# Issue order of the staged value stores, and the last output projection by heads, in a two-layer segment-memory transformer

## The chip, the cores and the metric

The kernel runs on one core of a Trainium2 chip. A core has four compute engines, each with its own instruction stream: PE (TensorE, matrix products into PSUM), DVE (VectorE), ACT (ScalarE) and POOL (GpSimd). A fifth engine, SP, does no arithmetic here: it issues most of the DMA transfers, one after the other. An instruction that waits for a semaphore holds up all that stands behind it on its own engine, and on no other. PE runs every product as a pair, a weight load (shown as PEld) and a matmul.

The metric is the device time of one execution in microseconds (us); shorter is better. The time before is 1611.96 us, the median of three runs (1608.64 to 1615.45).

## The reference

The input x has 2048 tokens of 512 features. Two layers, each applied twice in turn, make the output: A, a recurrent memory attention, and B, a dense block with ReLU, each behind a layer norm and with a residual.

```python
def _A_ref(x, mem0, Wq, Wk, Wv, Wo, seg_len):        # H=32 heads of 128, M=8, seg_len=32
    mem = mem0
    for s in range(n_seg):                             # 64 segments, one after the other
        h = concatenate([mem, xs], axis=1)             # 8 memory rows + 32 tokens
        q, k, v = h @ Wq, h @ Wk, h @ Wv               # per head
        p = softmax(where(mask, q @ k.T * scale, -1e9))
        o = (p @ v) summed over heads through Wo
        mem = o[:, :M, :]                              # the next segment's memory
        outs.append(o[:, M:, :])

x = x + A(layernorm(x), mem0, ...)
x = x + relu(layernorm(x) @ w1) @ w2                   # Dff = 1376
x = x + A(layernorm(x), mem0, ...)
x = x + relu(layernorm(x) @ w1) @ w2
```

The memory makes A sequential over its 64 segments. The second A needs the tokens of the first A and B only, so it may follow a few segments behind.

## The kernel before

**Steps.** One loop runs over steps k = 0 to 67 (`LAST`). Step k does segment k of the first A (k < 64) and segment k-4 of the second A (k >= 4, `DELTA`); B for the tokens of step k-2 is fitted in between. Steps 0 to 3 and 64 to 67 have one layer only (`single` in `step`); the others have both.

**Within a step.** For half of the heads `qk` makes queries and keys (L540, copied from PSUM by ACT at L546 and DVE at L548), `scores` (L574) and `softmax` (L590 to L606) follow, then the other half. `transpose_p` or a DMA transpose (`turn_p`, L623) turns the probabilities, `weighted_v` (L642) multiplies by the values in `Vs`, `output_mem` (L582) projects the memory rows, `new_memory` copies them (L774), turns them (L780) and hands them to the next step (`HTm` L791, `HT` L794). At the end `memory_values(k + 1)` makes the next step's values of the memory rows (L725), copies them (L729) and stores them.

**Values by way of DRAM.** The values of a segment's tokens do not depend on the memory and are made ahead, in `values0` (L314), `values_tile` (L354) and `memory_values` (L725). A product tile has heads across partitions, while `Vs` wants tokens there; so each tile is copied to SBUF (L320, L358, L729, all ACT), stored to DRAM in 128 KB pieces, and read back in the other layout (`load_values` L697 to L706, `load_memory_values` L735). The copies go to a ring of five SBUF buffers (tag `vst`): a copy must wait until the store of the copy five before it has landed.

**Step 0 and its staging.** Step 0 makes more value tiles than five buffers hold, while the weights still come in. It therefore puts 15 tiles into the space of the dense weights `w1_sb` and `w2_sb` (`slots` in `first_step`), which are loaded only in step 1 (`load_dense`, L157 to L160). The two stores of `vd_second` (L359), the values that step 1 needs, are issued at once. The other 13 go through `put(True, ...)`, which only appends them to the list `held`. Step 1 empties that list (L877) behind `load_memory_values` (L735) and ahead of its `load_dense`, which overwrites the staging space and so must wait for those stores.

**Order.** The streams of PE, DVE, SP and POOL are in the order in which the program is written. ACT's alone is arranged by a scheduler from its own estimates, so a change elsewhere can shift ACT's instructions.

**Output projection of the tokens.** `output_x(k)` multiplies the 32 token rows of all heads (`OTx`) by `Wo`. Four groups of 32 columns of the PE array work at once. In the quarter form (L401) the four groups take the four quarters of the 512 output columns of one head: 128 pairs of a weight load and a matmul of 128 columns. In the form by heads (L396, where `by_heads(k)` is true) they take two heads times two halves: 64 pairs with 256 columns each, and the two partial sums are added later: `add_output` then does four additions of 32x256 (L417) in place of four of 32x128 (L426). Before, `by_heads` is true for k = 0 to 2 and 63 to 65. The projection of step 67 is done after the loop, at the very end of the program, and has the quarter form.

Of the kernel before, what the change touches and what calls it, by code (L numbers as in the profile page):

```python
# [22 lines left out]
def kernel(  # L23
# [14 lines left out]
    nc = tc.nc  # L38
# [9 lines left out]
    LAST = NSEG + DELTA - 1  # L48
# [20 lines left out]
    def has0(k):  # L69
        return 0 <= k < NSEG  # L70

    def has1(k):
        return DELTA <= k <= LAST
# [30 lines left out]
    def load_xb(n):  # L104
        tag, bufs = ("vst", 5) if n in (1, 2, 3) else ("xb", 1)
        xbs[n] = wk.tile([128, Dm], BF, tag=tag, bufs=bufs, name="xb")
        nc.sync.dma_start(out=xbs[n][:], in_=A_x[0, 128 * n:128 * n + 128, :])
# [101 lines left out]
    for a in range(2):  # L209
        t = ps_s.tile([128, 512], F32, name=f"sp{a}")  # L210
# [4 lines left out]
    xT0, xnT_tiles, hT_tiles, vd0, vd1, vmds, wm_tiles, wo_tiles, xp_tiles, vp_tiles, obs = {}, {}, {}, {}, {}, {}, {}, {}, {}, {}, {}  # L215
# [9 lines left out]
    def normalize(eng, dst, src, mom, lo, hi):  # L225
        mv, rstd = mom
        eng.tensor_scalar(out=dst[lo:hi, :], in0=src[lo:hi, :], scalar1=mv[lo:hi, 0:1], scalar2=rstd[lo:hi, 0:1],
                          op0=ALU.subtract, op1=ALU.mult)

    def moments_x(n):  # L230
        stats = wk.tile([128, 6], F32, tag="ln_stats", bufs=1)
        nc.vector.bn_stats(out=stats[:], in_=xbs[n][:])
        return stat_tail(stats, "x")
# [47 lines left out]
    def layers(k):  # L281
        return [a for a in range(2) if (has0, has1)[a](k)]
# [10 lines left out]

    held = []

    def put(later, **store):
        if later:
            held.append(store)  # L300
        else:
            nc.sync.dma_start(**store)  # L302

    def values0(p, n, lo=0, hi=NC4, pool=None, stage=None):
        r = 64 * (p % 2)
        if (n, lo) == (0, 0):
            vd0[p] = dram.tile([4, 2, 64, 512], BF, tag="vd0", bufs=3, name="vd0")
        if lo == 0:
            pool, tag = (pool, "wo") if pool else (ps_fill, "fill")
            vp_tiles[p, n] = pool.tile([128, 512], F32, tag=tag, name="vp")  # L310
        vp = vp_tiles[p, n]
        for c4 in range(lo, hi):
            for j in range(2):
                nc.tensor.matmul(vp[64 * j:64 * j + 64, :], lhsT=xT0[p // 2][:, c4, r:r + 64],  # L314
                                 rhs=Wv_sb[:, c4, (n + j) * 512:(n + j + 1) * 512],
                                 start=(c4 == 0), stop=(c4 == NC4 - 1), tile_position=(0, 64 * j))
        if hi < NC4:
            return
        vst = wk.tile([128, 512], BF, tag="vst", bufs=5, name="vst")[:] if stage is None else stage
        nc.scalar.copy(out=vst, in_=vp[:])  # L320
        put(stage is not None, out=vd0[p][n // 2].rearrange("j t e -> (j t) e"), in_=vst)

    def values_first(ii):

# [78 lines left out]
                                     tile_position=(0, 32 * j))  # L403

    def by_heads(k):
        return k + 1 < LAST and len(layers(k + 1)) == 1

    def add_output(k, part=None):
        if not 0 <= k <= LAST or ox_span(k) is None:
# [306 lines left out]
    def memory_values(k, stage=(None, None), part=range(2)):  # L716
        if 0 in part:
            vmds[k] = dram.tile([2, 4, 32, 512], BF, tag="vmd", bufs=7, name="vmd")
        vmd = vmds[k]
        for ii in part:  # L720
            vp = ps_c.tile([128, 512], F32, tag="c", name="vm")
            for c4 in range(NC4):
                for j in range(4):
                    n = 4 * ii + j
                    nc.tensor.matmul(vp[32 * j:32 * j + 32, :], lhsT=HTm[:, c4, :],  # L725
                                     rhs=Wv_sb[:, c4, n * 512:(n + 1) * 512],
                                     start=(c4 == 0), stop=(c4 == NC4 - 1), tile_position=(0, 32 * j))
            VmS = wk.tile([128, 512], BF, tag="vst", bufs=5, name="VmS")[:] if stage[ii] is None else stage[ii]
            nc.scalar.copy(out=VmS, in_=vp[:])  # L729
            put(k == 0, out=vmd[ii].rearrange("j t e -> (j t) e"), in_=VmS)  # L730

    def load_memory_values(k, act):
        for ii in range(2):
# [23 lines left out]
    def split(k):  # L757
        return len(values_at(k)) in (2, 3)
# [90 lines left out]
    def step(k):  # L849
        act = layers(k)  # L850
        single = len(act) == 1
        cont = [a for a in act if k - DELTA * a + 1 < NSEG]
        n_x = k // 4 + 3
        has_x = n_x < NXT
        by_pe = k in (1, LAST)
        ahead = has1(k + 1) or not cont
        if k % 4 == 0 and has_x:
            load_xb(n_x)
        with tc.high_priority(offset=PRIO):
            behind = norm_rows.pop(k, None)  # L860
            if k == 1:
                def behind():
                    normalize(nc.vector, xbs[n_x], xbs[n_x], moments_x(n_x), 0, 128)
            qks = qk(0, act, behind=behind)
            load_values(k, act)
            if k == 1:
                memory_values(k)
                inputs_T(n_x, True)
        part = 4 if k == LAST else 8 if single else 5
        mid = 8 if k == LAST else 16  # L870

        light = split(k)
        block(k, 0, part)
        with tc.high_priority(offset=PRIO):
            transpose_step(k)
            load_memory_values(k, act)
            while held:  # L877
                put(False, **held.pop(0))
            scores(qks, act)
            softmax(0, act, by_pe)  # L880
            if not by_pe:
                turn_p()
        if k % 4 == 3 and has_x:
            inputs_T(n_x)
        if has0(k + 1):
            load_x(k + 1)
        if k == 1:
            load_dense()
        with tc.high_priority(offset=PRIO):
            qks = qk(1, act)  # L890
        if single:
            block(k, part, mid)
        elif light:
            dense_h(k - 2, slice(0, 1))
            block(k, part, 16)
        else:
            dense_h(k - 2)
        with tc.high_priority(offset=PRIO):
            scores(qks, act)
            softmax(1, act, by_pe)  # L900
        if single:
            dense_h(k - 2, slice(0, 1) if k == LAST else slice(None))
            block(k, mid, H)
        elif light:
            dense_h(k - 2, slice(1, None))
            block(k, 16, H)
        else:
            block(k, part, H)
        f_mid = 9 if ahead or k == 2 else 5
        if k < LAST:  # L910
            dense_y(k - 2, 0, f_mid)
        if not single:
            add_output(k - 1)
        if k % 4 == 1 and k > 1 and has_x:
            mom["x"] = moments_x(n_x)
        with tc.high_priority(offset=PRIO):
            transpose_p(1)
        if ahead and k < LAST:
            dense_y(k - 2, f_mid, NFC)
        tokens_in(k + 1)  # L920
        if k < LAST and spare_T(k + 1) is not None:
            nc.gpsimd.tensor_copy(out=HTm[:, :, 2 * M:32], in_=spare_T(k + 1))
        with tc.high_priority(offset=PRIO):
            pvs = weighted_v(act)
            outputs(k, pvs)
        if single and k < LAST and ahead:
            add_dense(k - 2)
            store(k - 2)
        if single:
            add_output(k - 1, 0)  # L930
        if cont:
            with tc.high_priority(offset=PRIO):
                pool, tag = (ps_c, "c") if single else (ps_wo, "wo")
                wo = pool.tile([128, Dm], F32, tag=tag, name="wo")
                output_mem(k, wo)
        if not ahead:
            dense_y(k - 2, f_mid, NFC)
        if not single and k < LAST and ahead:
            add_dense(k - 2)
            store(k - 2)  # L940
        if cont:
            with tc.high_priority(offset=PRIO):
                new_memory(k, cont, wo)
        if single:
            add_output(k - 1, 1)
        if not ahead:
            add_dense(k - 2)
            store(k - 2)
        values1(k + 1, 1)
        if cont:  # L950
            output_ride(k)
            with tc.high_priority(offset=PRIO):
                memory_values(k + 1)
        with tc.high_priority(offset=PRIO):
            prepare(k + 1)
        if k % 4 == 2 and k > 2 and has_x:
            normalize(nc.vector, xbs[n_x], xbs[n_x], mom["x"], 0, 128)

    mom = {}
    with tc.manual_schedule(engines={mybir.EngineType.PE, mybir.EngineType.DVE, mybir.EngineType.SP,  # L960
# [30 lines left out]
        t = xnT_tiles[d + 2] = wk.tile([128, NC4, 128], BF, tag="xnT", bufs=1, name="xnT")  # L991
# [48 lines left out]
```

## Time and profile before

| what | value |
|---|---|
| median of three runs | 1611.96 us (1608.64 to 1615.45) |
| the profiled execution's own time | 1608.92 us |
| its span, first to last instruction | 1607.2 us |
| mean granted TensorE clock | 0.995 |
| PE busy | 1570.6 us, 98% of the span, 42782 matmuls |
| DVE / ACT / POOL busy | 1262.9 / 738.7 / 347.6 us |
| DMA moved | 146.39 MB, mean 91 GB/s |

The span is 1.7 us shorter than the execution's own time. PE is close to always busy over the whole, so a saving can lie only where PE waits, or where PE's work itself shrinks. The timeline gives the start and length of each instruction or run of instructions, in us from the start of the span; a bracket behind a row says how long the engine had been idle and what ended that. In the chain of waits each row is a piece of the path that ended last.

### The profile page before, as it was taken

Reading aid. Unit: us, or ns where it says so; the run is one execution under the profiler, and the core shown is the slowest. Engines: PE = TensorE matmul, PEld = TensorE weight load, DVE = VectorE, ACT = ScalarE, POOL = GpSimd, SP = SyncE. Lnnn points to the kernel's source line nnn. Section 1 sums busy time; section 2 is a strip of 40 time slices with the busy share of each in tenths; the row PEclk is TensorE's granted clock in tenths of the full one; section 3 lists DMA queues with packets and bytes.
Section 4 is the critical chain, followed back from the end, with each engine's and each line's share of the span. In section 5 each row is a group of like instructions: output and inputs, shape, how many; then the busy total and the mean of one; then the engine's idle time right before and its main releaser. Section 6 shows DMA issues by size and latency. Waiting matters only on the chain.

```text
span 1607.2 us, 94867 instructions
## 1 busy us (share of the span) xinstructions
PE 1570.6 (98%) x42782; PEld 1324.2 (82%) x42782; DVE 1262.9 (79%) x3112; ACT 738.7 (46%) x1800; POOL 347.6 (22%) x666
## 2 busy tenths in 40 slices
PE   6889999999999999999999999999999999999997
PEld 4567888988898888889888888988888898888876
DVE  4468888888888888888888888888888888787765
ACT  3434445454544544454454545445454544545432
POOL 2012122222222222222222222222222222221210
PEclk9989999999999999999999999999999999999999
DMA  9634343444343355434433443343443333324232
GB/s 368 218 76 76 89 79 76 85 90 81 74 91 82 80 77 97 82 71 86 83 84 73 97 83 76 83 82 88 72 100 82 78 76 79 92 62 100 70 70 37
DMA packets 222533, 146.39 MB, mean 91 GB/s; under 512 B 123976, under 2 KB 216496, under 8 KB 222128
## 3 DMA queue, kind: packets, MB, share of 16 engines
q1 hardware_dynamic: 218976, 136.09, 38.3%
q8 instruction: 336, 5.51, 1.6%
q0 software_dynamic: 3072, 4.20, 1.1%
q14 instruction: 69, 0.57, 0.2%
q10 hardware_dynamic: 80, 0.03, 0.0%
HBM read 65.41 MB, written 45.35 MB: 69 GB/s over the span
## 4 chain that ended last, share of the span: by engine, by line
PE 94%; DMA 3%; SPq 1%; DVE 1%; issue 1%; ACT 0%; POOLq 0%; ACTq 0%; DVEq 0%
PE qp L540 37%; PE wox L373 10%; PE wo L582 8%; PE vm L725 7%; PE v L354 7%; PE hp L476 6%; PE sp L499 5%; PE pv L642 4%; PE sp L574 4%; PE vp L314 3%; DMA Wv_sb<-in_A_Wv_dram 2%; PE tp L616 1%; PE xp L447 1%; SPq L302 1%; DMA vd<-vst 0%
## 5 line engine op out<-in xcount | busy, mean ns | idle before, releaser
L546 ACT CAST QT<-qp 128x480 bf16<-128x480 f32 (+3 forms) x408 | 201.5, 494 | 395.7 <-PE qp L540 393.2
L540 PE MATMUL qp<-HT,Wk_sb 128*128 128x80 bf16 (+1 forms) x8704 | 369.8, 200 | 3.8 <-ACT VmS L729 2.3
L540 PE MATMUL qp<-HT,Wq_sb 128*128 128x80 bf16 (+1 forms) x8704 | 370.1, 200 | 2.4 <-POOL HT L714 1.2
L540 PEld LDWEIGHTS <-Wq_sb 128*128 128x128 bf16 x8704 | 326.2, 99 | 34.2 <-issue 26.7
L540 PEld LDWEIGHTS <-Wk_sb 128*128 128x128 bf16 x8704 | 328.9, 100 | 5.2 <-issue 4.0
L548 DVE CAST KT<-qp 128x480 bf16<-128x480 f32 (+3 forms) x408 | 225.3, 565 | 104.6 <-PE qp L540 102.3
L606 POOL TENSOR_TENSOR P_sb<-es,sm 128x320 bf16<-128x320 f32 x185 | 130.8, 721 | 753.4 <-ACT es L596 514.5
L373 PE MATMUL wox<-Wo_sb,OTx 128*64 128x256 bf16 x2880 | 173.8, 273 | 0.0
L590 DVE TENSOR_REDUCE mx<-sp 128x8 f32<-128x320 f32 x256 | 114.9, 487 | 74.1 <-PE sp L574 74.1
L601 DVE TENSOR_REDUCE sm<-es 128x8 f32<-128x320 f32 x256 | 118.9, 465 | 44.4 <-ACT es L596 34.0
L373 PEld LDWEIGHTS <-OTx 128*64 128x64 bf16 x2880 | 150.2, 110 | 3.1
L596 ACT ACTIVATE es<-es 128x320 f32<-128x320 f32 x256 | 110.5, 469 | 60.7 <-DVE es L594 59.9
L725 PE MATMUL vm<-Wv_sb,HTm 128*32 128x512 bf16 x2176 | 136.5, 380 | 0.6 <-DVE HT L794 0.6
L582 PE MATMUL wo<-Wo_sb,OTm 128*32 128x512 bf16 x2144 | 128.7, 380 | 0.0
L354 PE MATMUL v<-Wv_sb,xnT 128*32 128x512 bf16 x2048 | 128.7, 378 | 0.0
L566 DVE CAST sp<-maskb 128x320 f32<-128x320 bf16 x256 | 118.4, 484 | 0.0
L594 DVE TENSOR_TENSOR es<-sp,mx 128x320 f32<-128x320 f32 x256 | 113.8, 483 | 1.5
L725 PEld LDWEIGHTS <-HTm 128*32 128x32 bf16 x2176 | 91.0, 96 | 27.0 <-issue 12.4
L499 PE MATMUL sp<-w_sb,hT 128*64 128x256 bf16 (+4 forms) x1474 | 106.8, 278 | 0.5 <-ACT hT L482 0.5
L476 PE MATMUL hp<-xnT,w_sb 128*128 128x64 bf16 (+3 forms) x2948 | 102.8, 193 | 3.4 <-DMA xnT<-XN 2.4
L729 ACT CAST VmS<-vm 128x512 bf16<-128x512 f32 x134 | 78.6, 586 | 56.0 <-PE vm L725 53.9
L476 PEld LDWEIGHTS <-w_sb 128*128 128x128 bf16 (+1 forms) x2948 | 95.6, 101 | 4.5 <-issue 3.8
(113 smaller groups left out, 2026.4 us busy)
## 6 DMA issues: line engine op xcount, KB each, us to landing
Vs<-vd SPq DMA_DIRECT2D x96, 256.0 KB
vd<-vst SPq DMA_DIRECT2D x181, 128.0 KB
vmd<-VmS SPq DMA_DIRECT2D x134, 128.0 KB
Vs<-vmd SPq DMA_DIRECT2D x254, 32.0 KB
Vs<-vmd SPq DMA_DIRECT2D x60, 128.0 KB
Wq_sb<-in_A_Wq_dram SPq DMA_DIRECT2D x2, 2048.0 KB
Wk_sb<-in_A_Wk_dram SPq DMA_DIRECT2D x2, 2048.0 KB
Wv_sb<-in_A_Wv_dram SPq DMA_DIRECT2D x2, 2048.0 KB
```

Of the source, the lines that this page charges most:

```text
L354: nc.tensor.matmul(vp[32 * j:32 * j + 32, :], lhsT=tokens[:, c4, :], rhs=Wv_sb[:, c4, n * 512:(n + 1) * 512], start=(c4 == 0), stop=(c4 == ...
L373: nc.tensor.matmul(out[64 * j:64 * j + nr, 0:256], lhsT=lhsT, rhs=rhs[:, 256 * j:256 * j + 256], start=start, stop=stop, tile_position=(0, ...
L476: nc.tensor.matmul(hp[0:fs, fc - f0, 0:n], lhsT=w1_sb[:, c4, fc * 128:fc * 128 + fs], rhs=cols(c4), start=(c4 == 0), stop=(c4 == NC4 - 1))
L499: nc.tensor.matmul(sp_banks[bank][64 * j:64 * j + n, 0:w], lhsT=hT_tiles[d][0:fs, fc, 0:n], rhs=w2_flat[0:fs, fc * Dm + 256 * j:fc * Dm + ...
L540: nc.tensor.matmul(qp[:, hi, 0:ncol], lhsT=W_sb[:, c4, h * Dh:(h + 1) * Dh], rhs=HT[:, c4, a_lo:a_hi, :], start=(c4 == 0), stop=(c4 == NC4 ...
L546: nc.scalar.copy(out=dst[:, 0:nh, a_lo * L:a_hi * L], in_=qp[:, 0:nh, 0:ncol])
L548: nc.vector.tensor_copy(out=dst[:, 0:nh, a_lo * L:a_hi * L], in_=qp[:, 0:nh, 0:ncol])
L566: nc.vector.tensor_copy(out=sp_tiles[a], in_=maskb2)
L582: nc.tensor.matmul(wo[32 * j:32 * j + 32, :], lhsT=OTm[:, h, n, 2 * M * c:2 * M * c + 4 * M], rhs=Wo_sb[:, h, :], start=(h < 4), stop=(h > ...
L601: nc.vector.tensor_reduce(out=sm[:], in_=es[:], axis=AX.X, op=ALU.add)
L606: eng.tensor_tensor(out=P, in0=es[:], in1=sm[:].unsqueeze(2).to_broadcast([128, 8, L]), op=ALU.mult)
L725: nc.tensor.matmul(vp[32 * j:32 * j + 32, :], lhsT=HTm[:, c4, :], rhs=Wv_sb[:, c4, n * 512:(n + 1) * 512], start=(c4 == 0), stop=(c4 == NC ...
```

## The change

Two things are changed. First, `held` and `put` go: every store of a value tile is issued where its copy is written in the program. On SP the 13 stores of step 0 thus move from step 1 to step 0, ahead of the load of `Vs` from `vd_second` (L697), and `load_dense` follows directly on the loads of the memory values (L735) of step 1. The number of DMAs stays the same. Second, `by_heads` is true for the last step as well, so the projection after the loop takes the form by heads: 64 pairs on PE in place of 128, and four additions of 32x256 in place of four of 32x128 on DVE.

```diff
-    held = []
-
-    def put(later, **store):
-        if later:
-            held.append(store)
-        else:
-            nc.sync.dma_start(**store)
-
     def values0(p, n, lo=0, hi=NC4, pool=None, stage=None):
...
         nc.scalar.copy(out=vst, in_=vp[:])
-        put(stage is not None, out=vd0[p][n // 2].rearrange("j t e -> (j t) e"), in_=vst)
+        nc.sync.dma_start(out=vd0[p][n // 2].rearrange("j t e -> (j t) e"), in_=vst)
...
     def by_heads(k):
-        return k + 1 < LAST and len(layers(k + 1)) == 1
+        return k == LAST or k + 1 < LAST and len(layers(k + 1)) == 1
...
             nc.scalar.copy(out=VmS, in_=vp[:])
-            put(k == 0, out=vmd[ii].rearrange("j t e -> (j t) e"), in_=VmS)
+            nc.sync.dma_start(out=vmd[ii].rearrange("j t e -> (j t) e"), in_=VmS)
...
             load_memory_values(k, act)
-            while held:
-                put(False, **held.pop(0))
             scores(qks, act)
```

The program text of PE and DVE differs in that last projection and nowhere else. SP's order differs in the stores named. ACT's order, which the scheduler makes, differs in one more place: in step 2 the copy of the second tile of memory values (L729) stands right behind the first query copy (L546), where before it stood behind the third query copy of that half, the first of the next half and the exponential of the first half; and the second exponential stands behind the ReLU of the dense block (L482) rather than ahead of it. POOL's order is the same.

## The prediction

> **What bounds the kernel now.** The page comes first: PE carries 94% of the chain of waits, so only what PE itself waits for can be saved. Then that chain in order of time for the first 140 us, the one stretch where SP and DMA are long on it (start, length, what):
>
> ```profile
> PE 94%; DMA 3%; SPq 1%; DVE 1%; issue 1%; ACT 0%; POOLq 0%; ACTq 0%; DVEq 0%
> ```
>
> ```profile
> 57.56 1.81 DMA vmd<-VmS
> ...
> 59.72 0.34 SPq L302
> ...
> 64.61 0.45 SPq L302
> ...
> 66.09 2.29 SPq L302
> ...
> 73.24 7.47 DMA vd<-vst
> ...
> 80.73 0.59 ACT VmS L729
> ...
> 81.37 0.88 PE qp L540 x22
> 82.25 4.84 DMA xnT<-XN
> ...
> 87.13 1.55 PE hp L476 x44
> ```
>
> From 59.72 SP works off the 13 held stores (L302), most in 0.45 us, the slowest in 2.29. The first store of step 1's own copies (`vd<-vst`) goes out only at 73.24 and lands 7.47 us later, behind the dense weights; only then has ACT a buffer for the second `VmS` copy, at 80.73. SP itself stands behind that copy with its store, so the transpose of `XN` goes out at 82.25. PE's timeline shows the price in step 2 (71.63 to 98.15), and step 3, from 98.15, as the measure:
>
> ```profile
> 71.63 0.77 PE L540 MATMUL qp<-HT,Wq_sb 128*128 128x40 bf16 x24
> ...
> 75.79 0.25 PE L574 MATMUL sp<-KT,QT 128*40 128x40 bf16 x5
> 76.84 0.30 PE L574 MATMUL sp<-KT,QT 128*40 128x40 bf16 x11 [0.80 <-issue]
> ...
> 81.37 0.96 PE L540 MATMUL qp<-HT,Wk_sb 128*128 128x40 bf16 x24 [2.27 <-ACT VmS L729]
> ...
> 87.13 1.55 PE L476 MATMUL hp<-xnT,w_sb 128*128 128x32 bf16 x44 [2.38 <-DMA xnT<-XN]
> ...
> 91.67 0.48 PE L616 MATMUL tp<-ident,P_sb 128*64 128x80 bf16 x16
> ...
> 98.15 0.77 PE L540 MATMUL qp<-HT,Wq_sb 128*128 128x40 bf16 x24
> ...
> 102.15 0.46 PE L574 MATMUL sp<-KT,QT 128*40 128x40 bf16 x16
> ...
> 110.22 0.48 PE L616 MATMUL tp<-ident,P_sb 128*64 128x80 bf16 x16
> ```
>
> PE stands idle for 0.80, 2.27 and 2.38 us, and the view of stretches (PE, PEld, DVE, ACT, POOL busy, then granted clock, DMA share, GB/s) shows that the clock fell to about half behind the second of these:
>
> ```profile
> 75.00:80.00 5.00, 3.30 (x117) 2.83 (x114) 2.27 (x6) 0.77 (x2) 0.37 (x1) 1.00 1.03 343
> 80.00:85.00 5.00, 3.38 (x88) 2.79 (x88) 1.33 (x4) 1.14 (x3) 1.35 (x4) 0.56 0.91 137
> 85.00:90.00 5.00, 2.87 (x72) 2.50 (x75) 1.97 (x5) 1.16 (x4) 0.00 (x0) 0.50 0.40 65
> ```
>
> **Part one: the 13 stores move from step 1 to step 0.** The rows of the other engines that it touches:
>
> ```profile
> 43.84 0.83 SPq L359 DMA_DIRECT2D vd_second<-w_sb  x2
> 50.61 0.33 SPq L697 DMA_DIRECT2D Vs<-vd_second  x1
> 62.82 0.59 ACT L320 CAST vst<-vp 128x512 bf16<-128x512 f32 x1
> 65.52 0.57 PE L642 MATMUL pv<-PT,Vs 40*128 40x40 bf16 x16
> 68.96 0.39 SPq L157 DMA_DIRECT2D w_sb<-in_B_w_dram  x1
> 72.44 0.36 ACT L546 CAST QT<-qp 128x240 bf16<-128x240 f32 x1 [0.91 <-PE qp L540]
> 73.36 0.53 DVE L227 TENSOR_SCALAR XN<-R,mv,rstd 32x512 bf16<-32x512 f32 x1
> ```
>
> *Where the stores go.* SP is free of weight loads at 43.84. Fifteen stores at 0.45 us would end at 50.6, just where SP stood waiting before (L697 at 50.61). Some must wait for a completion count that an `Wo` load still in flight holds, so I put their end at 53, and L697, which also waits for the landing of the second `vd_second` store (now tenth), at 53 to 54. It is read by PE at 65.52: over 10 us of room. SP is in time for the next store, whose landing (57.56 + 1.81) sets the old order of SP. Price: nothing, and what covers it is that room.
>
> *Load of the dense weights.* L157 takes the place of the first held store: 59.72 for 68.96, 9.24 us earlier. The copy at 62.82 ends at 63.41, its store goes out directly, and behind the same loads it lands 9.24 us earlier too: 73.24 + 7.47 - 9.24 = 71.5.
>
> *The copy that waits for it.* The second `VmS` copy now stands on ACT right behind the first query copy of step 2, which ends at 72.44 + 0.36 = 72.8. The buffer is free by 71.5, so it waits for nothing, with 1.3 us to spare. Behind it on ACT stand the other query copies, and PE waits for those through PSUM: each us beyond the spare one is a us of PE.
>
> *What goes then.* The store of that copy leaves at 73.4, the load of `Vs` next, and the transpose, ready from `XN` at 73.36 + 0.53, at some 74.3. With the whole 4.84 us of before it lands at 79.1. I rebuild step 2: first scores at 75.79 as before; from there to the transposes of the second half as in step 3, 110.22 - 102.15 = 8.07, so 83.86 (the dense products stand at about 80.4, behind the landing at 79.1); then step 2's own end, 98.15 - 91.67 = 6.48, so 90.34. The gain is 98.15 - 90.34 = 7.8 us. It holds the idle times, the half clock and the 0.80 us of "issue", whose cause the trace doesn't name. Late next are the softmax of the second half, as in step 3, and the transposed probabilities.
>
> *What the moved traffic may cost.* 13 stores now run beside the end of step 0, and the dense loads beside step 1 instead of step 2. The nearest row is the 0.80 us at 76.84, beside loads at 343 GB/s. Bounds: once for each of the two stretches, 1.6 us, against nothing; a gain is excluded, since both stretches had less traffic before. I take 0.5, nearer to nothing, because step 1 has slack of its own while it waits for softmax and copies.
>
> **Part two: the last projection by heads.**
>
> ```profile
> 1591.53 1.62 PE L401 MATMUL wox<-Wo_sb,OTx 128*32 128x128 bf16 x101
> 1594.57 0.57 PE L401 MATMUL wox<-Wo_sb,OTx 128*32 128x128 bf16 x27 [1.42 <-issue]
> 1595.19 1.17 DVE L426 TENSOR_TENSOR R<-R,wox 32x128 f32<-32x128 f32 x4 [2.27 <-PE wox L401]
> 1599.03 0.34 PEld L995 LDWEIGHTS <-XN 128*128 128x128 bf16 x4 [0.41 <-DVE XN L227]
> ```
>
> ```profile
> 108.03 1.06 PE L396 MATMUL wox<-Wo_sb,OTx 128*32 128x256 bf16 x32
> ```
>
> ```profile
> 1574.24 0.86 DVE L417 TENSOR_TENSOR R<-R,wox 32x256 f32<-32x256 f32 x2
> ```
>
> ```profile
> q8 instruction: 336, 5.51, 1.6%
> ```
>
> PE now takes 1591.53 to 1595.14, 3.61 us, of which 1.42 is a stop after 101 pairs. By heads it is 64 pairs at 1.06/32 = 0.033 us: 2.1 us. The pairs as such are hardly shorter (3.61 less the stop is 2.2), so everything hangs on the stop. I read it as waiting for instructions: the instruction queue moves 5.51 MB in 336 packets, 16 KB each, some 280 instructions of the page's 94867, and short instructions use up such a packet fastest. With 64 pairs less, PE reaches that place in the dense products behind the projection, after 1594.57, when the packet is there. So PE gains 1.5. DVE's four additions take 4 x 0.43 = 1.72 for 1.17, all on the path, since L995 waits for `XN`, made from their sum: +0.55. Net -0.9. If the stop stays, it is +0.5.
>
> [...]
>
> **Sum.** -7.8 - 0.9 + 0.5 = -8.2 us. Against the profiled execution's own 1608.92 that is 1600.7. The median of the runs stands 3.0 above it; the mean of the three runs and this one is 1611.2, so for a median I give 1603.0.
>
> **Rivals.**
> *The buffer is late (part of the gain).* If the first `vst` store lands after 72.8, ACT stops ahead of the query copies, and PE with it. For it: only 1.3 us of room, and 15 stores ahead. Against it: the stores have some 6 us to drain ahead of 59.72. At 4 us late the sum is -4.2: 1607.0.
> *The loads of step 1 are late (slower).* L697 stands behind all 15 stores. If each held SP as long as the slowest did, 2.29 us, L697 would issue at 43.84 + 34.4 = 78.2 and land near 80 (as 1.81 for a store), 14.5 us after PE wants it at 65.52: -8.2 + 14.5 = +6.3, 1617.5. It decides from a landing at 73.7, or 1.9 us a store; over 0.5% slower from 2.4. For it: in step 0 the `Wo` loads are still in flight. Against it: 0.45 is the usual row.
> *The stop at the end stays.* -6.8: 1604.4. [...] Against it: a stop inside a run of equal instructions with no wait between them.
> *The change does not reach the path.* If step 2 stays as long because the transpose or the probabilities are late anyway, the time is within 2 us of before, about 1610. Against it: step 3 runs the same transfers without a PE wait.
>
> **How the numbers follow.** My forecast has 0.60, the late buffer 0.15, the stop that stays 0.08, no effect 0.09, the late loads 0.08. 0.5% of 1611.96 is 8.1 us, about what a measurement of this kernel can tell from no change, and puts the bound at 1603.9, close to the forecast: of the 0.60 I count 0.42 below it, and 0.02 of the stop's case: faster 0.44. Same is 0.18 + 0.06 + 0.15 + 0.08 + 0.02 = 0.49, slower 0.06 of the late loads and 0.01 of no effect: 0.07. The likeliest case alone runs from 1600 to 1606. The range reaches down to 1598.5 (the unknown traffic free, and a low set of runs) and up to 1610, past the late buffer and most of no effect.
>
> **What would show it.** In the new profile: L157 issued near 59.7 and the first `vst` store near 63.5; `VmS` copied right behind the first query copy without a wait for a DMA; no PE wait over 1 us between 71 and 91; clock 1.00 at 80 to 90; step 3's first queries at about 90.3; at the end 64 pairs in one run without a stop, and four additions of 0.43. It would be wrong with a wait for `Vs` at 65.5, for `VmS` at 73 to 76, or if step 2 is as long as before.

## The result and the profile after

The changed kernel takes 1603.65 us (median of 10 runs, 1601.33 to 1608.04) against 1611.86 us for the kernel before (10 runs, 1608.64 to 1615.45): a ratio of 0.9951, 95% interval 0.9939 to 0.9962, or 8 us less. The profiled execution took 1601.33 us, with a span of 1599.6.

In the changed kernel's text the lines behind the place of `held` have numbers that are lower by 8 to 10: L313 is the store of a `vst` copy, L721 the `VmS` copy, L722 its store, L532 the queries and keys, L468 the first dense product, L388 the projection by heads, L409 its additions, L393 the projection by quarters.

First the shares of the chain of waits, from the page of the profile after. The share of DMA and SP together fell from 4% to 3%, and PE rose by one:

```profile
PE 95%; DMA 2%; DVE 1%; SPq 1%; issue 1%; ACT 1%; POOLq 0%; ACTq 0%; DVEq 0%
```

Then SP's part of the timeline (start, length, engine, line, what, how many). The stores now run from 43.81 to 55.3, the dense weights (L157) follow on the loads of the memory values at 60.34, and the transpose of `XN` is issued at 74.27, where it was 82.25:

```profile
44.73 5.64 SPq L313 DMA_DIRECT2D vd<-w_sb  x6
...
51.45 3.81 SPq L313 DMA_DIRECT2D vd<-w_sb  x5
...
55.44 0.33 SPq L689 DMA_DIRECT2D Vs<-vd_second  x1
...
59.62 0.67 SPq L727 DMA_DIRECT2D Vs<-vmd  x2
...
60.34 1.09 SPq L157 DMA_DIRECT2D w_sb<-in_B_w_dram  x1
...
64.56 1.36 SPq L313 DMA_DIRECT2D vd<-vst  x3
...
71.50 2.08 SPq L722 DMA_DIRECT2D vmd<-VmS  x2
...
74.27 1.31 SPq L289 DMA_TRANSPOSE xnT<-XN  x1
```

Of PE's and ACT's timeline in step 2 these rows answer to the three stops shown of before. The second `VmS` copy has no bracket: it waits for nothing. `hp` (L468) has none either. Two stops for "issue" (idle time for which the profile names no releaser) are left, 0.35 and 0.16 us:

```profile
65.48 0.57 PE L634 MATMUL pv<-PT,Vs 40*128 40x40 bf16 x16
...
71.59 0.77 PE L532 MATMUL qp<-HT,Wq_sb 128*128 128x40 bf16 x24
...
72.39 0.36 ACT L538 CAST QT<-qp 128x240 bf16<-128x240 f32 x1 [0.91 <-PE qp L532]
72.65 0.59 ACT L721 CAST VmS<-vm 128x512 bf16<-128x512 f32 x1
...
79.30 0.43 PE L532 MATMUL qp<-HT,Wk_sb 128*128 128x40 bf16 x11 [0.35 <-issue]
...
80.52 1.34 PE L468 MATMUL hp<-xnT,w_sb 128*128 128x32 bf16 x44
...
83.57 0.71 PE L491 MATMUL sp<-w_sb,hT 128*32 128x256 bf16 x9 [0.16 <-issue]
...
90.68 0.77 PE L532 MATMUL qp<-HT,Wq_sb 128*128 128x40 bf16 x24
```

The view of stretches (PE, PEld, DVE, ACT, POOL busy, granted clock, DMA share, GB/s) shows full clock where it was 0.56 and 0.50:

```profile
80.00:85.00 5.00, 4.84 (x153) 3.96 (x142) 2.53 (x7) 1.46 (x5) 0.33 (x2) 1.00 0.81 72
85.00:90.00 5.00, 4.11 (x100) 2.36 (x100) 3.67 (x12) 1.28 (x5) 0.00 (x0) 1.00 0.00 0
```

From step 2's first queries to step 3's it is 90.68 - 71.59 = 19.09 us, before 98.15 - 71.63 = 26.52: 7.43 us shorter. The last projection starts at 1583.40, before at 1591.53, so steps 3 to 67 are 0.7 us shorter in this execution. Behind that start the new kernel is the slower one: 1599.6 - 1583.40 = 16.2 us to the end, before 1607.2 - 1591.53 = 15.7. The timeline and the stretches of that end:

```profile
1583.40 3.17 PE L388 MATMUL wox<-Wo_sb,OTx 128*32 128x256 bf16 x64
...
1586.61 1.76 DVE L409 TENSOR_TENSOR R<-R,wox 32x256 f32<-32x256 f32 x4 [1.82 <-PE wox L388]
```

```profile
1583.40:1586.60 3.20, 3.20 (x68) 2.35 (x68) 1.35 (x5) 0.16 (x1) 0.00 (x0) 0.58 0.02 5
...
1590.80:1594.30 3.50, 3.19 (x49) 2.92 (x50) 0.29 (x1) 1.14 (x4) 0.00 (x0) 0.52 0.01 2
```

The 64 pairs run without a stop, but at a granted clock of about half, and so do the last dense products.

### The profile page after: what moved, and what is told of

Its sections match the earlier page's. It is cut to its first block, busy times and chain, and to the rows that moved or that the text cites. A ratio compares the mean times of both kernels' runs of the same rounds, so it can differ in the third digit from the quotient of the medians.

```text
span 1599.6 us, 94752 instructions
## 1 busy us (share of the span) xinstructions
PE 1568.4 (98%) x42718; PEld 1323.1 (83%) x42718; DVE 1262.8 (79%) x3112; ACT 737.9 (46%) x1800; POOL 346.7 (22%) x666
## 4 chain that ended last, share of the span: by engine, by line
PE 95%; DMA 2%; DVE 1%; SPq 1%; issue 1%; ACT 1%; POOLq 0%; ACTq 0%; DVEq 0%
PE qp L532 37%; PE wox L365 10%; PE wo L574 8%; PE vm L717 7%; PE v L346 7%; PE hp L468 6%; PE sp L491 5%; PE pv L634 4%; PE sp L566 4%; PE vp L306 3%; DMA Wv_sb<-in_A_Wv_dram 2%; PE tp L608 1%; PE xp L439 1%; PE wox L388 1%; SPq L134 0%
## 5 line engine op out<-in xcount | busy, mean ns | idle before, releaser
L532 PE MATMUL qp<-HT,Wk_sb 128*128 128x80 bf16 (+1 forms) x8704 | 369.3, 199 | 2.3 <-DVE KT L540 1.3
L532 PE MATMUL qp<-HT,Wq_sb 128*128 128x80 bf16 (+1 forms) x8704 | 369.6, 200 | 1.5 <-POOL HT L706 1.2
L532 PEld LDWEIGHTS <-Wq_sb 128*128 128x128 bf16 x8704 | 326.1, 99 | 32.9 <-issue 25.6
L532 PEld LDWEIGHTS <-Wk_sb 128*128 128x128 bf16 x8704 | 328.5, 100 | 3.8 <-issue 2.7
L468 PE MATMUL hp<-xnT,w_sb 128*128 128x64 bf16 (+3 forms) x2948 | 103.4, 194 | 0.6 <-ACT xnT L986 0.3
L721 ACT CAST VmS<-vm 128x512 bf16<-128x512 f32 x134 | 78.4, 585 | 53.8 <-PE vm L717 53.8
L468 PEld LDWEIGHTS <-w_sb 128*128 128x128 bf16 (+1 forms) x2948 | 96.3, 101 | 1.8 <-issue 1.2
```

The source lines that it names most:

```text
L468: nc.tensor.matmul(hp[0:fs, fc - f0, 0:n], lhsT=w1_sb[:, c4, fc * 128:fc * 128 + fs], rhs=cols(c4), start=(c4 == 0), stop=(c4 == NC4 - 1))
L532: nc.tensor.matmul(qp[:, hi, 0:ncol], lhsT=W_sb[:, c4, h * Dh:(h + 1) * Dh], rhs=HT[:, c4, a_lo:a_hi, :], start=(c4 == 0), stop=(c4 == NC4 ...
```

## The experiments

Two theories of the gain in step 2. A: what counts is when SP comes past the 13 stores to the dense weights, because these weights fill the DMA engines for some 10 us (share 0.99 and 1.03 from 70 to 80 us in the kernel before), and all that step 2 needs then comes late. B: what counts is only the buffer, that is the second `VmS` copy, for which ACT and PE wait. Of the end of the kernel, the questions are whether the stop in the quarter form is a wait for PE's instructions, and where the gain of the shorter projection went.

**Each half alone.** The stores alone: `held` and `put` go, `by_heads` stays as before.

```diff
-            while held:
-                put(False, **held.pop(0))
```

> The stores of step 0 issued at once, the last projection in quarters as before. Theory A (the stores' place moves the dense loads some 9 us earlier, and with them the free buffer and the transpose of step 2): step 3's first queries at about 90.7 as in the changed kernel, time 7.5 us under before, ratio 0.995. Theory C (my prediction's second term: the projection by heads gives 0.9 us): this kernel is 0.9 us slower than the changed one. Against C, if the clock eats that term, it is as fast as the changed one or up to 0.5 us faster.

The heads alone:

```diff
-        return k + 1 < LAST and len(layers(k + 1)) == 1
+        return k == LAST or k + 1 < LAST and len(layers(k + 1)) == 1
```

> The projection by heads alone, the 13 stores held back as before. Theory A: step 2 as long as before (26.5 us), all of the gain gone, time within 1 us of before. Theory C: 0.9 us faster than before. By the clock of the changed kernel's end (half rate for 3.4 us inside the 64 pairs) the pairs take 0.05 us instead of 0.033 and the projection to the end of the span 15.7 to 16.2 us, nothing gained.

Stores alone: 1601.88 us against 1609.29 of before on the same chip, ratio 0.9953 (0.9941 to 0.9965). Heads alone: 1608.47, ratio 0.9994 (0.9986 to 1.0003). So the stores give the whole measurable gain; the heads give something between a gain of 2.3 us and a loss of 0.5. With the stores alone, L157 goes out at 59.47 and step 2 takes 19.58 us; with the heads alone, L157 goes out at 68.36 and step 2 takes 26.43, with the three stops of before in other sizes. PE's timeline with the heads alone:

```profile
77.34 0.30 PE L574 MATMUL sp<-KT,QT 128*40 128x40 bf16 x11 [1.30 <-issue]
81.00 0.96 PE L540 MATMUL qp<-HT,Wk_sb 128*128 128x40 bf16 x24 [1.08 <-ACT VmS L729]
86.05 1.55 PE L476 MATMUL hp<-xnT,w_sb 128*128 128x32 bf16 x44 [1.67 <-DMA xnT<-XN]
```

**The buffer alone.** The kernel before, with one edit: the second `VmS` copy of step 2 goes to a place of its own (space of `hT`, not in use then) and needs no store to land first.

```diff
-                memory_values(k + 1)
+                spare = wk.tile([128, NFC, 64], BF, tag="hT", ...)[:, 0:8, :]... if k == 1 else None
+                memory_values(k + 1, (None, spare))
```

> The kernel before, with the second copy of memory values for step 2 (L729) in a space of its own, the one that the dense block's hidden tile takes later, so that it needs no buffer of the ring; stores still held back. Theory B (all of the gain is that buffer): no PE wait for VmS, step 3 at about 90.7, 7.5 us faster. Theory A: the 2.3 us wait for VmS goes, but the transpose still stands behind the dense loads on the DMA engines and lands at 82 to 84 instead of 87.1, and the dense products wait for it: 3 to 5 us faster.

1607.35 us, ratio 0.9986 (0.9977 to 0.9995): 2 us, not 7.5, and less than the 3 to 5 that A gave. The wait for `VmS` is gone, and so, against A, is PE's wait for `xnT`; yet step 2 takes 23.78 us. PE's and SP's timeline of this run, the row of SP's waits (in all, times, longest) for the transpose, and the stretches:

```profile
76.89 0.30 PE L574 MATMUL sp<-KT,QT 128*40 128x40 bf16 x11 [0.77 <-issue]
...
82.81 0.53 PE L540 MATMUL qp<-HT,Wk_sb 128*128 128x40 bf16 x11 [2.53 <-issue]
```

```profile
68.26 0.38 SPq L157 DMA_DIRECT2D w_sb<-in_B_w_dram  x1
...
74.66 1.24 SPq L706 DMA_DIRECT2D Vs<-vd  x1
79.37 1.31 SPq L289 DMA_TRANSPOSE xnT<-XN  x1
```

```profile
SPq L289 <- DMA w_sb<-in_B_w_dram: 3.4, 1, 3.4
```

```profile
75.00:80.00 5.00, 4.24 (x161) 3.85 (x157) 2.53 (x8) 1.42 (x4) 0.31 (x1) 1.00 1.04 339
80.00:85.00 5.00, 2.47 (x65) 1.76 (x61) 1.12 (x4) 0.29 (x1) 1.40 (x4) 0.68 0.91 142
```

The transpose waits 3.4 us for the dense weights to land, as A has it. Behind 5 us with the DMA engines full (share 1.04, 339 GB/s) PE now stands 2.53 us for "issue" inside a run of equal products, and the clock is 0.68 in the mean from 80 to 85. B falls: without the buffer's wait, another effect of the same full DMA engines takes its place.

**A dose between.** The kernel before, with the 13 stores right behind the load of `Vs` (L697), so that SP meets them earlier than in the kernel before and later than in the changed one.

```diff
+            while held:
+                put(False, **held.pop(0))
...
-            while held:
-                put(False, **held.pop(0))
```

> The kernel before, with the 13 held stores issued right behind the load of Vs from vd_second (L697): seven us later than in the changed kernel, nine earlier than before. Theory A: the dense loads go out at 61 to 62.5 and the first vst store lands at 73 to 74, at most 1 us later than the VmS copy wants it: 6 to 7.5 us faster than before. If the early place in step 0 as such mattered, the gain would be about half.

1604.54 us, ratio 0.9967 (0.9954 to 0.9980): 4.75 us, less than the 6 to 7.5 of A and nearer to the half of the other reading. L157 goes out at 64.08, 1.6 us later than A allowed, and step 2 takes 22.22 us; two "issue" stops of 0.95 and 1.42 us stand in it. The first `vst` store lands only when the second `VmS` copy has waited 1.85 us for it on ACT, at 76.05. PE does not feel this wait, but SP does: it is held for 5.22 us at the store of `VmS` (L302, as in the kernel before), so that the transpose goes out at 77.54:

```profile
71.75 5.22 SPq L302 DMA_DIRECT2D vmd<-VmS  x2
...
76.05 0.58 ACT L729 CAST VmS<-vm 128x512 bf16<-128x512 f32 x1 [1.85 <-DMA vd<-vst]
...
77.54 1.30 SPq L289 DMA_TRANSPOSE xnT<-XN  x1
```

**Dense weights late, buffers early.** The changed kernel, with `load_dense` of step 1 moved behind the `vst` stores of that step, so that the weights come late and the buffers are free early.

```diff
-        if k == 1:
-            load_dense()
...
+        if k == 1:
+            load_dense()
```

> The changed kernel with the dense loads (L157 to L160) issued behind step 1's own vst stores, at about 65.3 instead of 60.3: the vst stores then land by 66 to 67 and no buffer is ever late. Theory A in its strict form (only the time of the dense loads counts; from the runs so far step 2 takes 19.1 us with the loads at 60.3, 22.2 at 64.1 and 26.5 at 69.0): step 2 takes about 23 us, 3.5 to 4 us of the gain lost. If it is what stands behind the loads that counts (the buffer, the transpose): no PE wait for VmS, the transpose is in time because the loads have landed by some 76, step 2 takes 19 to 20.5 us, at most 1.5 us slower than the changed kernel; what is lost are PE stops of about 0.8 us while instructions are fetched beside the loads.

1603.44 us against 1610.07, ratio 0.9965 (0.9953 to 0.9978). L157 goes out at 65.47, later than with the dose between, but step 2 takes only 20.19 us: the `VmS` copy waits for nothing, the transpose goes out at 73.81 and is in time. What is left of the price is one stop:

```profile
73.81 1.32 SPq L289 DMA_TRANSPOSE xnT<-XN  x1
...
77.12 0.30 PE L566 MATMUL sp<-KT,QT 128*40 128x40 bf16 x11 [1.50 <-issue]
```

So A in its strict form, by the time of the weights alone, falls too, and the second reading of the expectation holds. At nearly the same time of the weights (64.08 and 65.47) step 2 takes 22.22 and 20.19 us. Two things count: what stands behind the weights on SP (the `vst` stores, and through them the `VmS` copy and the transpose), and what shares the DMA engines with them (PE's instructions).

| run | L157 issued | PE's wait for `VmS` | transpose issued | "issue" stops of PE in step 2 | step 2 |
|---|---|---|---|---|---|
| before | 68.96 | 2.27 | 82.25 | 0.80 | 26.5 |
| heads alone | 68.36 | 1.08 | 81.86 | 1.30 | 26.4 |
| buffer alone | 68.26 | none | 79.37 | 0.77, 2.53 | 23.8 |
| shifted (below) | 66.79 | none | 81.19 | 1.58 | 23.0 |
| dose between | 64.08 | none | 77.54 | 0.95, 1.42 | 22.2 |
| weights late, buffers early | 65.47 | none | 73.81 | 1.50 | 20.2 |
| stores alone | 59.47 | none | 74.90 | 0.31, 0.34, 0.17 | 19.6 |
| changed | 60.34 | none | 74.27 | 0.35, 0.16 | 19.1 |

The second executions of the last two, told of below, take 18.7 and 18.9 us in step 2.

One thing varies with the rest and was not tested by itself: the place that the scheduler gives the second `VmS` copy on ACT. It stands ahead of the first query copy with the buffer alone and with the weights late, behind the first in the changed kernel, behind the second with the dose between, and behind the exponential in the kernel before. That place alone can hold SP. In the shifted run it is that of the kernel before; the copy waits for no DMA there, and yet comes only at 79.69, the transpose goes out at 81.19, and PE waits 1.91 us for `xnT`:

```profile
79.69 0.58 ACT L731 CAST VmS<-vm 128x512 bf16<-128x512 f32 x1
...
81.19 2.20 SPq L291 DMA_TRANSPOSE xnT<-XN  x1
```

So part of the gain of step 2 probably goes through this order, which came with the early stores. That is argued, for no run has the early stores with the old order.

**Where the stops fall.** If "issue" is a wait for the next packet of instructions, a stop must keep its place in PE's own count of instructions and shift in the program. The kernel before with 32 short pairs, that is 64 instructions of PE, added ahead of step 0; their result is overwritten.

```diff
+        for _ in range(16):
+            nc.tensor.matmul(t[:, 0:L], lhsT=ident[:], rhs=maskb[:], start=True, stop=True)
```

> The kernel before with 32 short pairs of a weight load and a matmul more at its very start (they fill the score bank that the mask overwrites), 64 PE instructions, early enough to cost nothing. If the stops named issue are PE waiting for the next packet of 256 instructions, all of them come 64 instructions earlier in the program: in the last projection the stop moves from behind pair 101 to behind pair 69, the one of 0.8 us in step 2 leaves the scores for the projection or the queries ahead of them. If they are tied to what the instructions do, they stay at pair 101 and at the scores. Time as before, within 1 us.

In the kernel before the last projection stops behind 101 of its 128 pairs. Here PE's timeline (the quarter form is L403 in this text) has the stop behind 69, which is 101 - 32:

```profile
1592.25 1.18 PE L403 MATMUL wox<-Wo_sb,OTx 128*32 128x128 bf16 x69
1594.42 1.02 PE L403 MATMUL wox<-Wo_sb,OTx 128*32 128x128 bf16 x59 [0.99 <-issue]
```

The first stop of step 2 shifts likewise, from the scores at 76.84 into the key products ahead of them:

```profile
76.50 0.43 PE L542 MATMUL qp<-HT,Wk_sb 128*128 128x40 bf16 x11 [1.58 <-issue]
```

In all the kernels the stops over 0.7 us in step 2 and in the last projection stand where the count of PE's instructions in the trace (weight loads, matmuls and semaphore instructions, up to the weight load behind the stop) leaves a remainder of 193 or 194 on division by 256. The 336 packets of the instruction queue hold 5.51 MB before, 16 KB each; PE's 86002 instructions in that trace are 256 for each of them.

The trace also has the start and length of each packet of that queue. Every one of these stops ends 1.2 to 1.6 us behind the end of a packet. By quarters PE works through the 256 instructions ahead of the last stop in 2.6 to 3.0 us, but from one such place to the next it takes 3.5 to 4.0: the next packet starts 1.1 to 1.2 us behind the stop, though the DMA engines are nearly idle (share 0.03). Beside the dense weights, in step 2 of before, of the heads alone and of the buffer alone (DMA share 0.98 to 1.08), it starts only 2.1 to 3.4 us behind the first stop. That is the way in which the full DMA engines held up PE here.

In the kernel before PE stood for more than 0.1 us at 8 of the 336 places with these remainders. At the stops over 0.7 us in step 2 and in the last projection, over all the kernels, crossing such a place cost 0.8 to 2.5 us. The time of the shifted run, 1608.86 us, lies inside the range of before (1607.06 to 1611.04 on that chip). Its step 2 is 3.5 us shorter than before, but its steps 3 to 67 are 4.3 us longer (1497.73 against 1493.38); the cause of that stays open, with one execution.

**The end, again and again.** The changed kernel was run twice more, the stores alone once more, and twice the changed kernel with five matmuls of 512 columns, whose result nothing reads, in the wait of PE ahead of `tpx`.

```diff
+        warm = ps_fill.tile([128, 512], F32, tag="fill", name="warm")
+        for _ in range(5):
+            nc.tensor.matmul(warm[:], lhsT=ident[:], rhs=Wq_sb[:, 0, 0:512], start=True, stop=True)
```

> The changed kernel once more, for a second sight of its end. [...] If the form by heads always draws the half clock onto itself, 3.2 us again.

> The changed kernel with five more matmuls of 512 columns, whose result nobody reads, in the 1.4 us in which PE waits for the normalized rows at the end. If it is that wait which halves the clock afterwards, the dense products behind it (44 pairs) take 1.7 us or less instead of 2.65, and the end comes 0.5 to 1 us sooner, counted from the start of the last projection. If the clock falls for another reason, nothing changes.

> The changed kernel a third time. If the half clock at the end is a matter of where the 3.41 us stretches begin: the way from the start of the last projection to the end of the span is 14.2 us when no stretch after it is at half clock (as in the runs with the late dense loads and with the extra matmuls), 15.5 to 16.2 when one or two are, and which of these it is follows from the place of the stretches: full clock when one begins 2.9 to 3.1 us behind the projection's start, half when one begins 0.5 to 1.9 us behind it.

> The stores alone once more: the last projection in quarters, with early stores. Step 2 19 to 20 us. Way from the start of the projection to the end of the span 14.5 to 14.9 us at full clock, 15.7 with one stretch at half clock; so the form by heads is worth 0.3 to 0.6 us at full clock and not the 0.9 of the prediction.

> The five extra matmuls in the wait at the end once more. If they keep the clock up, 14.2 us again wherever the stretches begin; if the first sight of it was luck, 15.5 to 16.2 when a stretch begins 0.5 to 1.9 us behind the projection's start.

The 3.2 us of the first of these texts is the length of the last projection, 3.17 in the changed kernel's first profile. In the order of these texts they took 1600.78, 1601.63, 1600.07, 1602.16 and 1602.73 us. Of every profile, the last projection, from its start to the end of the span, and the stretches of half clock in it (where a stretch begins, as us behind the start of the projection; those that begin behind PE's last product are left out):

| form | run | projection | to the end of the span | half clock from |
|---|---|---|---|---|
| quarters | before | 3.61 | 15.69 | 4.59 |
| quarters | stores alone, first | 3.06 | 14.77 | none |
| quarters | stores alone, second | 3.34 | 15.37 | 4.94 |
| quarters | buffer alone | 3.06 | 14.49 | none |
| quarters | dose between | 3.07 | 14.77 | none |
| quarters | shifted | 3.19 | 14.90 | none |
| heads | changed, first | 3.17 | 16.21 | 0.50 and 7.33 |
| heads | changed, second | 1.93 | 15.76 | 8.47 |
| heads | changed, third | 1.93 | 14.23 | none |
| heads | heads alone | 1.93 | 15.54 | 8.75 |
| heads | weights late | 1.93 | 14.24 | none |
| heads | with five matmuls, twice | 1.93 | 14.24, 14.23 | none |

In the quarter form the stop is there in all six runs, 0.87 to 1.42 us; by heads it is there in none. The same place of the changed kernel at full clock, in its third run, and the stop with the stores alone:

```profile
1584.13 1.93 PE L388 MATMUL wox<-Wo_sb,OTx 128*32 128x256 bf16 x64
...
1586.12 1.76 DVE L409 TENSOR_TENSOR R<-R,wox 32x256 f32<-32x256 f32 x4 [0.60 <-PE wox L388]
```

```profile
1584.77 1.62 PE L393 MATMUL wox<-Wo_sb,OTx 128*32 128x128 bf16 x101
1587.27 0.57 PE L393 MATMUL wox<-Wo_sb,OTx 128*32 128x128 bf16 x27 [0.87 <-issue]
```

At full clock the end takes 14.2 us by heads (two runs without the added matmuls) and 14.5 to 14.9 by quarters (four runs): 0.3 to 0.7 us less, 0.5 between the means. With half clock it takes 15.4 and 15.7 by quarters and 15.5 to 16.2 by heads. Over all runs without added matmuls the mean is 15.2 by heads (five) and 15.0 by quarters (six), so the gain of the heads is smaller than what the clock does to the end from run to run.

What decides on the half clock is not settled. It comes in stretches of 3.41 us, here and in step 2 of before (80.60 to 90.84, 10.24 us or three times that). In the trace of before, and in that after, all changes of the granted clock lie whole multiples of 3.413 us apart, from step 2 to the end (80.60 and 1596.12 in the trace of before: 444 times); boundaries are counted back by that. But where the stretches fall against the projection does not seem to decide by itself: heads alone has a boundary 1.92 us behind the projection's start (8.75 less two stretches) and a half stretch, the third run of the changed kernel has one at 1.97, counted back from a later half stretch, and none. PE's busy share of the stretch ahead doesn't either: half clock followed a share of 0.74 (first run of the changed kernel, 1580.49 to 1583.90) and one of 0.45 (its second run), full clock followed 0.46 (weights late) and 0.54 (third run of the changed kernel). The five matmuls were followed by full clock both times, which two of the five runs by heads without them had as well; they settle nothing.

## Why the prediction was right, and where it was not

*The time.* 1603.0 was forecast and 1603.65 measured; for the profiled execution 1600.7, and 1601.33. Of the sum of -8.2, step 2 with its traffic was to give -7.3 and gave -7.4, the end -0.9 and gave +0.5, and the steps between nothing and gave -0.7. The last two misses cancel in part, which is luck; step 2 is not.

*Where the stores go.* They end at 55.3, not 53: the eleven `vd` rows hold SP for 9.45 us, 0.86 each where 0.45 was the usual row. L697 (now L689) goes out at 55.44, 1.4 to 2.4 us late. The cover was read rightly: PE takes `Vs` at 65.48 without a wait. So the rival of the late loads did not come about.

*Dense weights.* L157 went out at 60.34, forecast 59.72. The first `vst` store was to follow the copy directly, near 63.5; it went out at 64.56, since SP was held for 2.43 us at the last of the dense loads (62.04 to 64.5). This step had 1.3 us of room for the buffer, and the two delays took a part of it that no row here gives; the copy at 72.65 still waited for nothing.

*The copy, the transpose, step 2.* Forecast and measured: transpose issued 74.3 and 74.27; dense products at 80.4 and 80.52; step 3's first queries at 90.34 and 90.68. No wait over 1 us between 71 and 91, and clock 1.00. The shares of the 7.8 us weren't told apart in the forecast, and the runs show why the whole had to be taken as one: with the buffer alone the wait for `VmS` goes (2.27 us), and 2.53 us of "issue" come. The prediction had ACT's new order right and built on it; what that order gives by itself was not measured.

*The moved traffic.* 0.5 us was the term, and 0.35 + 0.16 of "issue" is there, but in step 2, when the dense weights are through (DMA share 0.40, 94 GB/s from 75 to 80), and not beside step 1's loads. That the size agrees is luck in part: with the stores alone the three stops sum to 0.8, and in the second execution of that kernel one of 0.2 is left.

*The last projection.* This is the step that was mis-sized. Its mechanism holds: the stop is a wait for PE's instructions, it goes with 64 pairs fewer (none in seven runs by heads, 0.87 to 1.42 in six by quarters), and DVE's additions take 1.76 for 1.17 (forecast 1.72). The "some 280 instructions" a packet were those of all engines together; PE's own give 256. But the term -0.9 was made from the stop of one execution, 1.42, the longest of the six; the shortest, 0.87, came in three of them. With it the projection goes from 3.06 to 1.93 at full clock, -1.1, and with DVE's +0.6 the term is -0.5, as the ways to the end of the span have it in the mean. And the granted clock at the end was taken as given: in the execution profiled after, two half stretches in place of one made the end 0.5 us longer than before instead of shorter. The heads alone, 0.9986 to 1.0003, contain both -0.9 and nothing.

*The rest.* 0.7 us came between step 3 and the last projection, forecast as nothing. It is not to be put down to the change: that way takes 1493.38 us before and 1492.72, 1492.66 and 1493.63 in the three executions of the changed kernel, so three executions of one program differ by more. Before, step 67 has "issue" stops of 1.0 us in all; the second and third executions of the changed kernel have 1.2 and 1.4 there, the first less than 0.1.

*The rival of the stop that stays.* No run by heads has the stop (none in seven). The shifted run speaks against the rival too (69 pairs in place of 101), and so do the packets that end 1.4 to 1.6 us ahead of where PE goes on.

## What to carry to other kernels

In the kernel before the dense weights filled the DMA engines (share 0.99 and 1.03 from 70 to 80 us), and that their data are wanted late did not make them free of cost. See what else must come through the same engines while such a block runs: here a small store that frees a buffer (7.47 us to its landing in the kernel before), a transpose (waited 3.4 us for the weights with the buffer alone) and the instructions of the busiest engine (stops of 0.8 to 2.5 us). Put the block where nobody waits for these. When a wait is removed alone and the time hardly moves, look for the wait that took its place before concluding that the wait was harmless. A term read from one stop in one execution needs a second execution: the stop at the end ranged from 0.87 to 1.42 us, and the clock moved the end by up to 2 us.

## What was not expected of the hardware

Data transfers held up PE's supply of instructions: beside the dense weights PE stood 0.8 to 2.5 us for the next 256, and with DMA engines nearly idle (share 0.03) still 0.9 to 1.4 us where it ran through pairs of 128 columns in 16 ns each (1.62 us for 101 pairs), since the next 256 instructions came only after 3.5 to 4.0 us. The mark of it here was a stop for "issue" in the middle of equal instructions that kept its place in PE's count and not in the program: behind 69 pairs in place of 101 with 32 pairs added ahead.

The clock at the end of the same program differed between executions: none, one or two half stretches of 3.41 us, worth up to 2.0 us (14.23 to 16.21) of a kernel of 1600.
